# Joining the retention matmul clusters of three more groups, and splitting the last group's stores over two queues, in a retention layer followed by a squared-ReLU MLP

## The chip, the cores and the metric

The kernel runs on one core of one Trainium2 chip. The metric is the device time of one launch in microseconds (us), as the median over runs. A span is the part of one profiled execution between its first and last recorded work.

## What is computed

The first half is retention, that is, attention without a softmax and with a causal decay mask; the second half is an MLP with a squared ReLU. All inputs and the output are float32.

```python
# q, k, v: (8, 8, 576, 64); w_in: (512, 2048); w_out: (2048, 512)
scores = (1/sqrt(64)) * q @ k.T                       # per batch and head
gamma  = 1 - 2.0**(-5 - arange(8))                    # one decay per head
D      = where(rel >= 0, gamma**rel, 0)               # rel = row - column
x      = (scores * D) @ v                             # heads joined: (4608, 512)
h      = x @ w_in
out    = (maximum(h, 0)**2) @ w_out                   # (4608, 512)
```

## The kernel before

**Tiling.** The 4608 rows are cut into 36 units of 128 rows. A "full" unit is one chunk of 128 positions of one batch; a "tail" unit holds the last 64 positions of two batches. Two units make a group, so there are 18 groups, numbered 0 to 17; groups 8 and 17 are tails. Units 0 to 7 (groups 0 to 3, `PAIRED = 8`) take another path, with transposes on TensorE; from group 4 on, the two projections `kq` of a unit (k and q, cast to fp16 on POOL at L371 and L382) are transposed by a DMA into the tile `kqT` (L400, in `fx2`). The values are cast and scaled on POOL into `v16` (L387).

**Retention.** For each group there are four sets of small 64x64 matmuls on TensorE, all issued by the helper `quad` (L357): the scores (tile `psc`), the sum of k times v over the chunk, for the running state (`psS`), the contribution of the earlier state to the output (`psO`, from `kqT` and the states `R` and `Rm`; `emit_out1`), and the contribution of the chunk itself (`psO`, from the masked scores `rT` and `v`; `emit_out2`). VectorE masks the scores into `rT` (L692), updates the state (L711 to L717 and L461), and scales `psO` into `xT`, the input of the MLP (L751).

These sets stand on TensorE in two ways, which `add_ret` chooses by `joined(g)`, that is, `JOIN <= g < last_g` with `JOIN = 7`.

- Not joined: one cluster `fa` (scores and sums of the group), and later one cluster `fb` (`emit_out1`, an explicit `nc.tensor.drain()`, `emit_out2`).
- Joined: one cluster `f1` (`emit_out1` of group g and the scores of group g+1), and later one cluster `f2` (the sums of group g+1 and `emit_out2` of group g). So the scores of group g+1, and with them the transposed tiles `kqT` of its two units, are needed when the output of group g is made.

**MLP.** The first product is 64 matmuls of 128x256 per group (L875, tile `ph`). ScalarE applies the ReLU (L883, `rl`), ScalarE or VectorE squares it (L893, L895, `gT`). The second product is made from seven half-size products instead of eight (L972, tiles `po`; 56 matmuls of 128x256 per group), with sums of `gT` on VectorE (L945, `gS`) and sums of the results on ScalarE and VectorE (L985, L995, L1013, L1024, L1046) into the output tile `o`. The output of a group is stored by `store` on SP's queue (L845, L849); loads of q, k and v are on SP's queue as well (L298, L301, L304). A load needs one of five slots `ld`, which its casts free.

**Order.** The order of all instructions comes from a planner in the kernel (`Schedule`). Each task has an engine, a key (a lower key goes first among ready tasks), an assumed duration, dependencies and buffers. The planner plays through the program with these durations and emits the instructions in the order of its starts; on the chip each engine then works through its own list in that order and waits at semaphores. A changed duration, key or dependency can therefore reorder everything that follows. The key of the casts of a group depends on `JOIN` too: they are due one or two times `L = 32` ahead of the group.

**The last group.** Group 17 stores four halves of 128x256, each as two DMAs of 64 rows (one for each of two batches): the halves that the tasks `d11` and `d22` finish on ACT's queue, those of `c12` and `d21` on SP's. `d21` (L995) is the last to finish.

Of the kernel before, what the change touches and what calls it, by code (L numbers as in the profile page):

```python
# [15 lines left out]
class Schedule:  # L16
# [7 lines left out]
    def add(self, eng, key, dur, fn, deps=(), acq=(), after=None, lag=0.0):  # L24
        t = dict(eng=eng, key=key, dur=dur, fn=fn, acq=acq, n=len(self.tasks), users=[], free=[], lag=lag,
                 left=len(deps), ready=0.0, lat=self.LAT[eng] if after is None else after)
        for d in deps:
            d["users"].append(t)
        self.tasks.append(t)
        return t  # L30
# [73 lines left out]
def kernel(  # L104
# [9 lines left out]
    nc = tc.nc  # L114
    B, H, S, D = q.shape
    DM, DFF = w_in.shape
    assert (B, H, S, D, DM, DFF) == (8, 8, 576, 64, 512, 2048)
    P = 128
# [114 lines left out]
    WT_KEY = 96  # L233
    URGENT = 40
    SQ_LATE = (1, 4, 6)
    JOIN = 7
    LAG = {"k4": 0.7, "q4": 0.5}
    LAG_T, LAG_O = 1.5, 5.0
    PAIRED = 8
# [3 lines left out]
    add = sched.add  # L243
# [105 lines left out]
    T = {}  # L349
# [15 lines left out]
    def add_unit(u, base):  # L365

        kind, b, c = units[u]
        tail = [tail_dec] if kind == "tail" else []

        def sorted_cast(op, out_, in_):  # L370
            op(out=out_.rearrange("p (n b a d) -> p n b a d", n=2, b=2, a=2),  # L371
               in_=in_.rearrange("p (a n b) d -> p n b a d", n=2, a=2))

        def fk():
            t = tile_of["kq", u] = cast.tile([P, 2, H * D], FP16, name="kq16", tag="kq16")
            sorted_cast(nc.gpsimd.tensor_copy, t[:, 0], tile_of["k32", u])

        def fq():
            if kind == "tail":
                sorted_cast(nc.gpsimd.tensor_copy, tile_of["kq", u][:, 1], tile_of["q32", u])  # L380
            else:
                nc.gpsimd.tensor_copy(out=tile_of["kq", u][:, 1].rearrange("p (t a d) -> p a t d", t=4, a=2),  # L382
                                      in_=tile_of["q32", u].rearrange("p (a t) d -> p a t d", a=2))

        def fv():
            t = tile_of["v16", u] = cast.tile([P, H, D], FP16, name="v16", tag="v16")
            nc.gpsimd.tensor_tensor(  # L387
                out=t, in0=tile_of["v32", u],
                in1=vdec[kind].rearrange("p (h o) -> p h o", o=1).to_broadcast([P, H, D]), op=ALU.mult)
        ck = add("POOL", base, 0.65, fk, deps=[loaded["k", u]], acq=("kq",))  # L390
        cq = add("POOL", base + 1, 0.62, fq, deps=[loaded["q", u], ck])
        cv = add("POOL", base + 2, 1.1, fv, deps=[loaded["v", u]] + tail, acq=("v16",))
        for what, t in (("k", ck), ("v", cv)):
            for w in gate.get((what, u), []):
                sched.need(w, t)
        T["casts", u] = [ck, cq, cv]
        sched.free("ld", [ck, cq, cv])
        def fx2():
            t = tile_of["kqT", u] = work.tile([P, 2 * NP, P], FP16, name="kqT", tag="kqT", bufs=6)
            nc.sync.dma_start_transpose(out=t, in_=tile_of["kq", u].rearrange("p x n -> p (x n)"))  # L400
        T["kqT", u] = [add("SP", -1, 2.7, fx2, deps=[ck, cq], acq=("kqT",), after=3.0, lag=LAG_T)]

    def add_unit_pair(u, base):

# [180 lines left out]
    def units_of(g):  # L585
        return sorted(groups[g])
# [4 lines left out]
    def base_of(g):  # L591
        return (units_of(g)[0] - len(groups[g])) * L - EARLY
# [81 lines left out]
    def joined(g):  # L674

        return JOIN <= g < last_g

# [83 lines left out]
    def add_casts(g):  # L761
        for u in units_of(g):
            if u < PAIRED:
                if u % 2 == 0:
                    add_unit_pair(u, base_of(g) - 5)
                continue
            add_unit(u, base_of(g) - L * (2 if g > JOIN else 1) + 4 * (u - units_of(g)[0]))

# [50 lines left out]
    HF, HM = NF // 2, DM // 2  # L819
# [18 lines left out]
                sched.need(w, p)  # L838
    wT_done = {7: t3, 6: t2, 5: t1, 4: t4}

    def store(u, o, lo=0, hi=DM, eng=nc.sync):
        kind, b, c = units[u]
        if kind == "full":
            r0 = b * S + c * P
            eng.dma_start(out=out[r0:r0 + P, lo:hi], in_=o[:, lo:hi])  # L845
        else:
            for i in range(2):
                r0 = (b + i) * S + 512
                eng.dma_start(out=out[r0:r0 + 64, lo:hi], in_=o[i * 64:(i + 1) * 64, lo:hi])  # L849


    T["ff2"] = []
# [4 lines left out]
    def add_ff(g):  # L857
# [45 lines left out]
        if STRASSEN <= g:  # L903
            add_strassen(g, us, base2, sq)
            return
        ends = []
        for s, u in enumerate(us):
            end = base2 + NF * (s + 1)
            f2 = []
            late = g == 0 and s == 1  # L910
            for fi in range(NF):
                def f(fi=fi, s=s, u=u):
                    if fi == 0:
                        tile_of["po", u] = ps_ff.tile([P, DM], FP32, name="po", tag="ff")
                    nc.tensor.matmul(tile_of["po", u], lhsT=tile_of["g", g][:, fi, s * P:(s + 1) * P],  # L915
                                     rhs=w_out16[:, fi, :], start=(fi == 0), stop=(fi == NF - 1))
                f2.append(add("PE", 95.9 + fi / 1000 if late else base2 + NF * s + fi, 0.216, f, deps=[sq[fi // nf]] + wcast[4 + fi // 4] + f2[-1:],
                              acq=("ff",) if fi == 0 else ()))

            def fo(u=u):  # L920
                tile_of["o", u] = o_pool.tile([P, DM], FP32, name="o", tag="o")
                nc.scalar.copy(out=tile_of["o", u], in_=tile_of["po", u])
            oc = add("ACT", end + 1, 0.59, fo, deps=[f2[-1]], acq=("o",))
            sched.free("ff", [oc])
            st = add("SP", -0.5, 0.7, lambda u=u: store(u, tile_of["o", u]), deps=[oc], after=2.5, lag=LAG_O)
            sched.free("o", [st])
            ends.append(f2[-1])
# [3 lines left out]
    def add_strassen(g, us, base, sq):  # L931
# [56 lines left out]
        def o_tile(u):  # L988
            if ("o", u) not in tile_of:
                tile_of["o", u] = o_pool.tile([P, DM], FP32, name="o", tag="o")  # L990
            return tile_of["o", u]

        def on_dve_add(u, half, x, name, key, deps, acq=()):
            def f():
                nc.vector.tensor_tensor(out=o_tile(u)[:, half * HM:(half + 1) * HM], in0=bank(x), in1=tile_of[name, g],  # L995
                                        op=ALU.add)
            return add("DVE", base + key - URGENT, 0.42, f, deps=deps, acq=acq)

        if g == last_g:
# [17 lines left out]
            d11 = on_dve_add(uA, 0, "b", "p1", 17, [p2, c1, c12])  # L1017
# [8 lines left out]
            d22 = on_dve_add(uB, 1, "c", "u4", 21, [p7, c4], ("o",))  # L1026
            d7 = add("DVE", base + 22, 0.42, f7, deps=[d22, c2], acq=("p1",))
            d21 = on_dve_add(uB, 0, "e", "p1", 29, [p4, d7])
        else:
# [6 lines left out]
            d11 = on_dve_add(uA, 0, "b", "p1", 17, [p2, c1], ("o",))  # L1036
# [4 lines left out]
            d22 = on_dve_add(uB, 1, "c", "u4", 22, [p7, c4], ("o",))  # L1041
# [14 lines left out]
        for u, ds in ((uA, [d11, c12]), (uB, [d22, d21])):  # L1056
            if g < last_g:
                st = [add("SP", -0.5, 0.7, lambda u=u: store(u, o_tile(u)), deps=ds, after=2.5, lag=LAG_O if g < last_g - 1 else 0.0)]
            else:
                st = []  # L1060
                for d in ds:
                    lo = 0 if d in (d11, d21) else HM
                    eng = ("ACT", base + 25.1, 0.05) if d is d11 or d is d22 else ("SP", -0.5, 0.05)
                    st.append(add(*eng, lambda u=u, lo=lo, eng=eng: store(u, o_tile(u), lo, lo + HM,
                                                                          nc.scalar if eng[0] == "ACT" else nc.sync),
                                  deps=[d], after=2.5))
            sched.free("o", st)

    for g in range(len(groups)):
# [42 lines left out]
```

## Time and profile before

| | |
|---|---|
| Median of 4 runs | 290.21 us (290.06 to 290.32) |
| The profiled execution: its own time | 290.32 us |
| The profiled execution: span | 288.6 us |
| TensorE (PE) busy | 280.6 us, 97% |
| PE weight load (PEld) busy | 236.1 us, 82% |
| ScalarE (ACT) busy | 187.9 us, 65% |
| VectorE (DVE) busy | 179.0 us, 62% |
| GpSimd (POOL) busy | 89.0 us, 31% |

The profiled execution's own time is 1.7 us above its span: work that lies before and after what is recorded. Busy times of TensorE are modelled at their ends, since matmuls overlap. In a chain or a timeline the first two columns are the start and the length in us; then come the engine, the line and what was written from what; "x8" is the number of instructions.

### The profile page before, as it was taken

How to read it: one execution, taken by the hardware profiler on the slowest of the kernel's cores; microseconds unless marked ns; L12 is line 12 of the kernel's file. 1: busy time of each engine (PE TensorE's matmuls, PEld its weight loads, DVE VectorE, ACT ScalarE, POOL GpSimd, SP SyncE). 2: the span in 40 equal slices, each digit the busy share in tenths (PEclk: the TensorE clock that was granted, in tenths of full speed). 3: DMA queues.
4: the chain of work that ended last, by engine and by line, in shares of the span. 5: the costliest groups of instructions: out<-in, count | busy, mean ns of one | idle time of the engine just before them, and what ended most of it. 6: DMA issues, size and time to landing. Idle time of an engine off the chain costs nothing.

```text
span 288.6 us, 10134 instructions
## 1 busy us (share of the span) xinstructions
PE 280.6 (97%) x4346; PEld 236.1 (82%) x4346; DVE 179.0 (62%) x341; ACT 187.9 (65%) x363; POOL 89.0 (31%) x124
## 2 busy tenths in 40 slices
PE   6999999999999999999999999999999999999994
PEld 2568767888888888888888888888888888888883
DVE  3772389757574848737677676666457656265632
ACT  5559975767575767567676757584867585847830
POOL 5660046433514336252525154262433000000000
PEclk9999999999999999999999999999999999999999
DMA  7999999998989898999989799979989010202004
GB/s 201 275 208 206 249 287 273 196 236 145 237 204 228 179 232 200 210 196 240 155 216 200 169 180 224 214 174 234 174 209 193 2 73 2 75 2 75 0 9 139
DMA packets 122156, 49.94 MB, mean 173 GB/s; under 512 B 94720, under 2 KB 117760, under 8 KB 122112
## 3 DMA queue, kind: packets, MB, share of 16 engines
q1 hardware_dynamic: 117568, 44.84, 70.8%
q0 software_dynamic: 4224, 4.19, 8.8%
q8 instruction: 34, 0.56, 0.8%
q10 hardware_dynamic: 320, 0.26, 0.4%
q14 instruction: 10, 0.08, 0.1%
HBM read 36.70 MB, written 9.44 MB: 160 GB/s over the span
## 4 chain that ended last, share of the span: by engine, by line
PE 91%; DMA 3%; POOL 2%; issue 2%; DVE 0%; POOLq 0%; DVEq 0%
PE ph L875 44%; PE po L972 36%; PE psO L357 4%; DMA w_in<-in_moe_w_in_dram 3%; PE po L915 2%; PE psc L357 2%; PE psS L357 2%; PE psT L439 1%; POOL mask L216 0%; POOL vx L420 0%; POOL w_in L331 0%; DVE o L995 0%; POOL mask_full L208 0%; POOL mask_tail L208 0%; DVE p L1024 0%
## 5 line engine op out<-in xcount | busy, mean ns | idle before, releaser
L875 PE MATMUL ph<-xT,w_in 128*128 128x256 f16 x1152 | 138.4, 273 | 0.1
L875 PEld LDWEIGHTS <-w_in 128*128 128x128 f16 x1152 | 111.3, 98 | 14.5 <-DMA w_in<-in_moe_w_in_dram 0.4
L883 ACT ACTIVATE rl<-ph 128x512 f16<-128x512 f32 x144 | 84.5, 588 | 56.2 <-PE ph L875 53.7
L893 ACT ACTIVATE gT<-rl 128x512 f16<-128x512 f16 x118 | 74.7, 633 | 3.4
L972 PEld LDWEIGHTS <-gS 128*128 128x128 f16 x544 | 51.7, 98 | 6.5
L972 PE MATMUL po<-wT,gS 128*128 128x256 f16 x408 | 55.9, 273 | 0.0
L972 PEld LDWEIGHTS <-gT 128*128 128x128 f16 x408 | 39.7, 98 | 4.7
L945 DVE TENSOR_TENSOR gS<-gT,gS 128x512 f16<-128x512 f16 (+1 forms) x51 | 31.9, 626 | 18.3 <-ACT gT L893 17.7
L972 PE MATMUL po<-w_out,gT 128*128 128x256 f16 x272 | 36.7, 273 | 0.0
L371 POOL CAST kq<-k 128x512 f16<-128x512 f32 x28 | 20.7, 740 | 45.2 <-DMA k<-in_k_dram 41.3
L387 POOL TENSOR_TENSOR v<-v,vdec_full 128x512 f16<-128x512 f32 x24 | 26.7, 1112 | 23.4 <-DMA v<-in_v_dram 18.8
L945 DVE TENSOR_TENSOR gS<-gT 128x1024 f16<-128x1024 f16 x34 | 26.6, 782 | 10.8 <-ACT gT L893 10.7
L382 POOL CAST kq<-q 128x512 f16<-128x512 f32 x24 | 16.1, 672 | 31.2 <-DMA q<-in_q_dram 31.1
L895 DVE TENSOR_TENSOR gT<-rl 128x512 f16<-128x512 f16 x26 | 11.9, 458 | 21.5 <-ACT rl L883 21.5
L995 DVE TENSOR_TENSOR o<-po,u 128x256 f32<-128x256 f32 x33 | 13.9, 422 | 17.1 <-PE po L972 8.4
L985 ACT COPY u<-po 128x256 f32<-128x256 f32 x34 | 12.5, 369 | 13.6 <-PE po L972 13.5
L751 DVE TENSOR_TENSOR xT<-psO,gam_full 128x512 f16<-128x512 f32 x28 | 18.0, 684 | 3.7 <-PE psO L357 3.5
L995 DVE TENSOR_TENSOR o<-po,p 128x256 f32<-128x256 f32 x18 | 7.6, 424 | 19.2 <-ACT u L985 10.0
L972 PE MATMUL po<-w_out,gS 128*128 128x256 f16 x136 | 17.8, 273 | 0.0
L972 PE MATMUL po<-wT,gT 128*128 128x256 f16 x136 | 17.6, 273 | 0.0
L692 DVE TENSOR_TENSOR rT<-psc,mask_full 128x512 f16<-128x512 f32 x24 | 15.7, 683 | 2.1 <-PE psc L357 2.0
L461 DVE TENSOR_TENSOR R<-stmp,dec 128x512 f16<-128x512 f32 (+1 forms) x18 | 12.1, 672 | 0.4
(82 smaller groups left out, 220.4 us busy)
## 6 DMA issues: line engine op xcount, KB each, us to landing
out_dram<-o SPq DMA_DIRECT2D x32, 256.0 KB, 2.6
k<-in_k_dram SPq DMA_DIRECT2D x24, 256.0 KB, 5.2
q<-in_q_dram SPq DMA_DIRECT2D x96, 64.0 KB, 3.3
v<-in_v_dram SPq DMA_DIRECT2D x24, 256.0 KB, 4.2
pair<-in_k_dram SPq DMA_DIRECT2D x4, 512.0 KB, 8.0
pair<-in_q_dram SPq DMA_DIRECT2D x4, 512.0 KB, 5.5
pair<-in_v_dram SPq DMA_DIRECT2D x4, 512.0 KB, 7.3
w_in<-in_moe_w_in_dram POOLq DMA_DIRECT2D x4, 512.0 KB, 8.9
```

What stands on the lines that cost most here:

```text
L357: t = nc.tensor.matmul(out_, lhsT=lhsT, rhs=rhs, start=start, stop=True, skip_group_check=True, tile_position=(64 * row, 64 * col))
L371: op(out=out_.rearrange("p (n b a d) -> p n b a d", n=2, b=2, a=2), in_=in_.rearrange("p (a n b) d -> p n b a d", n=2, a=2))
L382: nc.gpsimd.tensor_copy(out=tile_of["kq", u][:, 1].rearrange("p (t a d) -> p a t d", t=4, a=2), in_=tile_of["q32", u].rearrange("p (a t) d ...
L387: nc.gpsimd.tensor_tensor(out=t, in0=tile_of["v32", u], in1=vdec[kind].rearrange("p (h o) -> p h o", o=1).to_broadcast([P, H, D]), op=ALU. ...
L692: tile_of["masking", g] = nc.vector.tensor_tensor(out=tile_of["rT", g][:, :, a], in0=tile_of["psc", g][a].rearrange("p (s n i) -> p s n i" ...
L751: nc.vector.tensor_tensor(out=tile_of["x", g].rearrange("p n (s e i) -> p e (n s) i", s=n, e=2)[:, c], in0=y.rearrange("p (o t r) -> p o r ...
L875: nc.tensor.matmul(tile_of["ph", g, fb][:, j, :], lhsT=w_in16[:, m, fi * P:(fi + 1) * P], rhs=tile_of["x", g][:, m, :], start=(m == 0), st ...
L883: nc.scalar.activation(out=t, in_=tile_of["ph", g, fb], func=ACTF.Relu)
L893: nc.scalar.activation(out=t, in_=rl, func=ACTF.Square)
L945: nc.vector.tensor_tensor(out=tile_of["S", g][:, k, sl], in0=in0(sl), in1=in1(sl), op=op)
L972: nc.tensor.matmul(tile_of["pb", g, bank], lhsT=left(i), rhs=right[:, i, :], start=(start and i == 0), stop=(i == HF - 1), skip_group_chec ...
L995: nc.vector.tensor_tensor(out=o_tile(u)[:, half * HM:(half + 1) * HM], in0=bank(x), in1=tile_of[name, g], op=ALU.add)
```

## The change

There are three edits.

1. `JOIN` goes from 7 to 4. Groups 4, 5 and 6 are now joined as well. Three clusters `fa` (of groups 5, 6, 7) and three clusters `fb` (of groups 4, 5, 6) become three `f1` and three `f2`. The same small matmuls are issued in them; three explicit drains are gone. The casts of groups 5, 6 and 7 are keyed earlier by 32.
2. The planner counts a DMA transpose as 2.1 us of SP's time instead of 2.7. The transposes themselves are the same.
3. Each of the last group's four half stores has its first DMA on SP's queue and its second on ACT's, instead of both on one of them. There are eight DMAs as before, four on each queue.

```diff
-    JOIN = 7
+    JOIN = 4
...
-        T["kqT", u] = [add("SP", -1, 2.7, fx2, deps=[ck, cq], acq=("kqT",), after=3.0, lag=LAG_T)]
+        T["kqT", u] = [add("SP", -1, 2.1, fx2, deps=[ck, cq], acq=("kqT",), after=3.0, lag=LAG_T)]
...
-    def store(u, o, lo=0, hi=DM, eng=nc.sync):
+    def store(u, o, lo=0, hi=DM, engs=(nc.sync, nc.sync)):
         kind, b, c = units[u]
         if kind == "full":
             r0 = b * S + c * P
-            eng.dma_start(out=out[r0:r0 + P, lo:hi], in_=o[:, lo:hi])
+            engs[0].dma_start(out=out[r0:r0 + P, lo:hi], in_=o[:, lo:hi])
         else:
             for i in range(2):
                 r0 = (b + i) * S + 512
-                eng.dma_start(out=out[r0:r0 + 64, lo:hi], in_=o[i * 64:(i + 1) * 64, lo:hi])
+                if engs[i]:
+                    engs[i].dma_start(out=out[r0:r0 + 64, lo:hi], in_=o[i * 64:(i + 1) * 64, lo:hi])
...
                 for d in ds:
                     lo = 0 if d in (d11, d21) else HM
-                    eng = ("ACT", base + 25.1, 0.05) if d is d11 or d is d22 else ("SP", -0.5, 0.05)
-                    st.append(add(*eng, lambda u=u, lo=lo, eng=eng: store(u, o_tile(u), lo, lo + HM,
-                                                                          nc.scalar if eng[0] == "ACT" else nc.sync),
-                                  deps=[d], after=2.5))
+                    for i, eng in enumerate((("SP", -0.5, 0.05), ("ACT", base + 25.1, 0.05))):
+                        engs = (nc.sync, None) if i == 0 else (None, nc.scalar)
+                        st.append(add(*eng, lambda u=u, lo=lo, engs=engs: store(u, o_tile(u), lo, lo + HM, engs), deps=[d], after=2.5))
```

## The prediction

> **What bounds the kernel now.** I read the page's busy row and its slices first, then TensorE's waits, then the chain of work that ended last, then TensorE's timeline around the clusters that the change touches, and last SP's and ACT's timelines at the end.
>
> ```profile
> PE 280.6 (97%) x4346; PEld 236.1 (82%) x4346; DVE 179.0 (62%) x341; ACT 187.9 (65%) x363; POOL 89.0 (31%) x124
> PE   6999999999999999999999999999999999999994
> ```
>
> TensorE is busy in all slices but the first and the last. Its waits between 20 and 284 us come back as an empty list, and the chain of that stretch stays on it. So a microsecond is gained only by what TensorE itself does, or by what follows its last matmul. The chain prices a cluster. First group 5, not joined, then groups 7 and 8, joined:
>
> ```profile
> 75.01 1.75 PE po L972 x16
> 76.75 0.38 PE psc L357 x32
> 77.42 0.54 PE po L972 x4
> ...
> 80.14 1.75 PE ph L875 x16
> 82.24 0.57 PE psO L357 x48
> 82.81 0.98 PE po L972 x8
> ...
> 126.01 0.87 PE ph L875 x8
> 127.39 1.85 PE po L972 x16
> 129.24 1.75 PE ph L875 x16
> 131.37 0.40 PE psO L357 x48
> 131.76 2.73 PE ph L875 x24
> ```
>
> A wide matmul streams in 0.1092 us (1.75/16). A cluster costs the gap between the wide matmuls on its two sides, plus what the first wide batch after it takes too long. `fa`: 76.76 to 77.42 is 0.66, and four matmuls in 0.54 instead of 0.44 add 0.10: 0.76. `fb`: 81.89 to 82.81 is 0.92, plus 0.11: 1.03. `f1` (126.88 to 127.39, plus 0.10): 0.61. `f2` (130.99 to 131.76, plus 0.11): 0.88. The timeline shows why `fb` is dear:
>
> ```profile
> 81.95 0.19 PE L357 MATMUL psO<-kqT,R 64*64 64x64 f16 x1
> 82.24 0.32 PE L357 MATMUL psO<-rT,v 64*64 64x64 f16 x16
> ...
> 113.49 0.19 PE L357 MATMUL psO<-kqT,R 64*64 64x64 f16 x1
> 113.51 0.43 PE L357 MATMUL psc<-kqT 64*64 64x64 f16 x32
> ```
>
> The first pair is `fb` of group 5: after the last matmul of `emit_out1` the explicit drain holds the next start back by 0.29. The second is `f1` of group 7: the scores follow after 0.02, since they use other banks and need no drain.
>
> The end, SP's timeline and then ACT's, each for its last issues:
>
> ```profile
> 284.91 1.11 SPq L849 DMA_DIRECT2D out_dram<-o  x2
> 283.12 1.20 ACTq L849 DMA_DIRECT2D out_dram<-o  x2
> 284.36 1.25 ACTq L849 DMA_DIRECT2D out_dram<-o  x2
> ```
>
> The last half (`d21`, 284.45 plus 0.42) is ready at 284.87. SP issues its two DMAs one after the other: the first takes 0.47, the second starts near 285.44, and the tile view gives 2.0 to 2.1 us from an issue to its landing.
>
> **What the Trainium skill says.** "TensorEngine Tiling (Array Packing)", Key Properties: changing the tiling mode drains TensorE. The trace agrees: each way back from 64x64 to full matmuls costs the 0.10 to 0.11 above. Joining leaves two clusters for a group, so this part is not saved. "DMA: Bandwidth & Descriptors", Rules for kernel authors: spreading DMAs over queues gives no bandwidth and saves only the sequencer's issue time. The trace has that time: 0.47 to 0.59 on SP, 0.56 to 0.61 on ACT. "Perfetto Trace Analysis", What "DMA-bound" means: one form is an issuing sequencer that is solid with DMA slices. SP is nearly so from 50 to 80 us here; rival C rests on it. The same page, Optimizing Scalar/DVE Operations: GpSimd and VectorE share an SBUF read port. A `gS` of 128x1024 takes 0.69 alone and 1.40 at 66.74, beside a POOL product at 66.55.
>
> **The change, part by part.**
>
> *Clusters.* Removed: three `fa` at 0.76 (2.28) and three `fb`, of groups 4, 5 and 6, which cost 1.00, 1.03 and 1.04 by the same reading (3.07): 5.35 us. Added: three `f1` at 0.61 and three `f2` at 0.88: 4.47. Gain **0.88**, all on the path, as TensorE has no idle time. Bounds: 0.75 (group 4 has no earlier state, so its clusters are shorter in both forms) and 1.0.
>
> *What the new places ask for.* In the changed program's order, `fa` of group 4 stays, and the wide matmuls between the clusters can be counted: 92 up to `f1` of group 4, 30 up to its `f2`, then 54, 32, 68, 32 and 68. With 0.1092 each, the cluster costs above and 62.64 as the start (62.54 plus the 0.10), `f1` of groups 4 to 7 begin at 72.7, 83.3, 95.7 and 108.2. They need the `kqT` of units 11, 13, 15 and 17 (each the later of a pair). In the trace of before these are issued at 66.39, 77.29, 89.73 and 103.23, and a transpose lands 3.4 to 4.0 (median 3.7) later: 70.1, 81.0, 93.4 and 106.9. **They are in time by 2.6, 2.3, 2.3 and 1.3 without being moved at all.** In SP's new order a k load (0.58, for the tail 1.46) stands ahead of the second transpose of three of these pairs, and stores (0.5 each) go behind it, so it comes at most about a microsecond later than before: still in time. POOL's order there is unchanged, and v of units 11, 13 and 15, which `f2` needs, was cast by 67.6, 78.5 and 91.6, against `f2` at 76.6, 87.4 and 99.8. So nothing is charged; if this cover fails, `f1` waits on TensorE with all wide matmuls behind it.
>
> *VectorE's hand-over.* `f2` waits for the masks of the next group: two of 0.64, that is 1.29, with 3.3 us (30 wide matmuls) for them in the tightest place, group 4. After `f2` of group 4, 22 wide matmuls (2.40 us) precede the first `ph` that needs its `xT`; before, that lead was over 9 us. The two `xT` take 1.28 together. With one or two `gS` ahead of them, at 0.69 to 1.40, the wait lies between 0 and about 0.5. I take 0, because the `gS` can run while `f2` does; both ends go into the range. Joined groups 7 to 16 run today with no TensorE wait, with the same banks held.
>
> *Transposes at 2.1.* A planner's number: no instruction changes, and what it moves is counted above. Later `f1` have more lead, as the transposes then run ahead of need.
>
> *Stores.* The four DMAs on ACT and four on SP remain. SP now also waits for `d11` and `d22`, and ACT for `c12` and `d21`; behind these waits stand only further last stores, since ACT's last copy (L1013) is already done. ACT's part of `d22` (ready 284.01) would be issued by 284.65, so it is free at 284.87. Both DMAs of `d21` then start near 284.91 instead of 284.91 and 285.44. Gain **0.5**. Bounds: 0 (they share 16 engines, and the second lands when it did) and 0.6.
>
> *Sum.* 0.88 + 0.5 = 1.38. The profiled execution took 290.32, so 288.94; its time is 0.11 above the median 290.21, against which the sum gives 288.83. I say **288.9**.
>
> **The rivals.**
>
> *A, the forecast (75%): 288.9*, by itself 288.5 to 289.3.
>
> *D (11%): the stores gain nothing*, because the last landing is set by what the engines do with 128 KB at once, not by the second issue. The DMA share is only 0.5 to 0.85 between 285 and 287 us, which speaks against it. 290.21 - 0.88 = 289.3.
>
> *B (7%): small VectorE stalls.* At `f2` of group 4 the plan leaves less than before, and POOL's casts of unit 13 fall in it. Two stalls of 0.4 take 0.8 of 1.38: 289.6, which is about no change. Against it: VectorE is 62% busy.
>
> *C (7%), slower: the transposes become the bound.* From 50 to 80 us SP issues almost without a pause, and the 16 DMA engines' share is 1.0. If the k load ahead of a transpose (256 KB, 1.3 us at the stretch's 207 GB/s) and slow q loads (3.4 instead of 2.1 us of SP, both seen) add up, `f1` stands and TensorE with it. It decides once the transposes come more than 2.3 us later than before; the gain is gone at 3.7, and it is slower by over 0.2% from about 4.3. At 5 us late: 2.7 of waits, 290.21 - 1.38 + 2.7 = 291.5. Against it: SP's list up to unit 13 is almost the same, so only something not seen in the trace makes it so late. That the change doesn't join anything is ruled out by the built order.
>
> **How the numbers follow.** About 0.2% (0.58 us) is what can be told from no change here. Faster by more than that are A and D, 86%; within it B, 7%; slower C, 7%. The range of 288.4 to 289.7 takes A with the bounds of the clusters, the hand-over and the stores, and most of D and B; C stays out.
>
> **What would show it.** Right: in the chain, clusters near 0.61 and 0.88 for groups 4 to 6, no pause of 0.29 after `emit_out1`, TensorE's waits still empty, last issues of SP and ACT both near 0.04 after the last `o`, and the end 0.5 nearer to it. Wrong: a TensorE wait for `kqT` near 73, 83, 96 or 108 us (C), or for `xT` near 80 us (B), or the tail from the last `o` to the end still 3.7 us (D).

## The result and the profile after

| | before | after |
|---|---|---|
| Median, us | 290.30 (52 runs, 289.88 to 291.49) | 291.40 (32 runs, 289.89 to 294.76) |
| The profiled execution: own time | 290.32 | 291.77 |
| The profiled execution: span | 288.6 | 290.1 |
| Last `o` written, from the span's start | 284.87 | 286.44 |

The ratio of after to before is **1.0034**, with an interval of 1.0022 to 1.0046: slower by a third of a per cent, about 1 us. The change was forecast to gain 1.4. (Ratios here leave out disturbed runs, so they aren't the quotients of the medians.) After scatters more than before.

The busy row, TensorE's slices and the chain's shares from the page of after:

```profile
PE 281.4 (97%) x4346; PEld 236.0 (81%) x4346; DVE 178.7 (62%) x341; ACT 188.4 (65%) x363; POOL 89.1 (31%) x124
PE   7999999999999997999999999999999999999994
...
PE 57%; DMA 19%; SPq 13%; DVE 3%; POOL 2%; issue 2%; ACT 1%; POOLq 0%; DVEq 0%
```

The busy row is nearly that of before. The slices show one new 7, the sixteenth, from 108.8 to 116.0 us. The chain has changed most: TensorE held 91% of it before, now 57%, and DMA with SP's issuing hold 32%. TensorE's waits over the whole span (total, times, longest) name what it waits for:

```profile
PE psc L357 <- DMA kqT<-kq: 1.8, 2, 1.6
```

Its timeline shows the two places. They are the scores in `f1` of group 7 and in `f1` of group 8; the bracket gives the idle time and what ended it:

```profile
108.53 0.30 PE L357 MATMUL psc<-kqT 64*64 64x64 f16 x16
110.46 0.32 PE L357 MATMUL psc<-kqT 64*64 64x64 f16 x16 [1.63 <-DMA kqT<-kq]
...
122.93 0.30 PE L357 MATMUL psc<-kqT 64*64 64x64 f16 x16
123.40 0.32 PE L357 MATMUL psc<-kqT 64*64 64x64 f16 x16 [0.17 <-DMA kqT<-kq]
```

The first unit's 16 scores run, the second unit's `kqT` isn't there yet, and all wide matmuls stand behind it. By the prediction's reading (the gap between wide matmuls plus the first batch's excess) these clusters cost 2.42 and 0.97 instead of 0.60. SP's timeline has the transpose that group 7 waits for, of unit 17:

```profile
103.08 1.33 SPq L400 DMA_TRANSPOSE kqT<-kq  x1
104.46 0.58 SPq L301 DMA_DIRECT2D k<-in_k_dram  x1
105.16 1.52 SPq L400 DMA_TRANSPOSE kqT<-kq  x1
```

It is issued at 105.16 (103.23 before), and its scores begin at 110.46: 5.3 us later.

The clusters of the newly joined groups are as forecast. Group 5 in TensorE's timeline, `f1` and then `f2`:

```profile
82.27 1.26 PE L876 MATMUL ph<-xT,w_in 128*128 128x256 f16 x10
83.61 0.43 PE L357 MATMUL psc<-kqT 64*64 64x64 f16 x32
83.97 1.05 PE L973 MATMUL po<-w_out,gS 128*128 128x256 f16 x8
...
85.72 1.91 PE L876 MATMUL ph<-xT,w_in 128*128 128x256 f16 x16
87.56 0.45 PE L357 MATMUL psS<-v,kq 64*64 64x64 f16 x32
...
88.34 0.72 PE L876 MATMUL ph<-xT,w_in 128*128 128x256 f16 x5
```

The ten `ph` end at 82.27 + 10 x 0.1092 = 83.36 and the next wide matmul starts at 83.97: 0.61 from these rounded starts. The 16 `ph` end at 87.47 and the next starts at 88.34: 0.87. There is no pause of 0.29.

**The books of the profiled execution.** The last `o` is 1.57 later. The six clusters of groups 4 to 6 cost 0.59, 0.85, 0.60, 0.87, 0.71 and 0.88, together 4.50, against 5.35 before: -0.85. `f1` of group 7 adds 1.82 and that of group 8 0.37. One hole of 0.19 at 77.9, where TensorE waits for a `gS`, is new. That is +1.53; the rest, 0.04, is scatter of single clusters. The tail after the last `o` is 0.07 shorter, so the span grows by 1.5.

### The profile page after: what moved, and what is told of

The parts are those of the page before. It is cut to its first block, busy times and chain, and to the rows that moved or that the text cites. A ratio compares the mean times of both kernels' runs of the same rounds, so it can differ in the third digit from the quotient of the medians.

```text
span 290.1 us, 10131 instructions
## 1 busy us (share of the span) xinstructions
PE 281.4 (97%) x4346; PEld 236.0 (81%) x4346; DVE 178.7 (62%) x341; ACT 188.4 (65%) x363; POOL 89.1 (31%) x124
## 4 chain that ended last, share of the span: by engine, by line
PE 57%; DMA 19%; SPq 13%; DVE 3%; POOL 2%; issue 2%; ACT 1%; POOLq 0%; DVEq 0%
PE ph L876 27%; PE po L973 25%; DMA pair<-in_v_dram 6%; SPq L298 5%; DMA w_out<-in_moe_w_out_dram 5%; DMA k<-in_k_dram 3%; DMA kqT<-kq 3%; DMA q<-in_q_dram 2%; SPq L316 2%; PE psO L357 2%; SPq L304 2%; SPq L400 2%; SPq L301 1%; PE psS L357 1%; DMA v<-in_v_dram 1%
## 5 line engine op out<-in xcount | busy, mean ns | idle before, releaser
L876 PE MATMUL ph<-xT,w_in 128*128 128x256 f16 x1152 | 136.4, 273 | 0.0
L946 DVE TENSOR_TENSOR gS<-gT,gS 128x512 f16<-128x512 f16 (+1 forms) x51 | 31.0, 607 | 20.3 <-ACT gT L894 19.6
L387 POOL TENSOR_TENSOR v<-v,vdec_full 128x512 f16<-128x512 f32 x24 | 27.6, 1150 | 23.9 <-DMA v<-in_v_dram 19.9
L371 POOL CAST kq<-k 128x512 f16<-128x512 f32 x28 | 19.2, 687 | 29.6 <-DMA k<-in_k_dram 27.6
L986 ACT COPY u<-po 128x256 f32<-128x256 f32 x34 | 12.6, 370 | 20.3 <-PE po L973 20.1
L896 DVE TENSOR_TENSOR gT<-rl 128x512 f16<-128x512 f16 x26 | 12.6, 483 | 19.3 <-ACT rl L884 19.3
```

What stands on the lines that cost most here:

```text
L387: nc.gpsimd.tensor_tensor(out=t, in0=tile_of["v32", u], in1=vdec[kind].rearrange("p (h o) -> p h o", o=1).to_broadcast([P, H, D]), op=ALU. ...
L876: nc.tensor.matmul(tile_of["ph", g, fb][:, j, :], lhsT=w_in16[:, m, fi * P:(fi + 1) * P], rhs=tile_of["x", g][:, m, :], start=(m == 0), st ...
L946: nc.vector.tensor_tensor(out=tile_of["S", g][:, k, sl], in0=in0(sl), in1=in1(sl), op=op)
```

## The experiments

All were timed beside the kernel before. The edits are against before or after, as named.

### Which edit loses: each alone

**Stores alone** (edit 3 on the kernel before; here against after, with edits 1 and 2 taken back):

```diff
-    JOIN = 4
+    JOIN = 7
...
-        T["kqT", u] = [add("SP", -1, 2.1, fx2, ...
+        T["kqT", u] = [add("SP", -1, 2.7, fx2, ...
```

> The kernel before with the third edit alone: the last group's half stores with one DMA on each queue. Theory T (late transposes make the changed kernel slower, the stores are nearly neutral): 290.1 to 290.3, ratio 0.999 to 1.000, and a tail from the last o to the end within 0.1 us of the 3.73 of before, as in the changed kernel's 3.66. Rival S (the forecast's store gain is there and was hidden): 289.8, ratio 0.998, tail about 3.2.

Measured: 0.9992 (0.9983 to 1.0002), about 0.2 us, and not told from nothing. The tail from its last `o` to the end is 3.6. Up to the end this is the program of before, so its profile is a second execution of the same order; it is used below.

**Transposes at 2.1 alone** (edit 2 on the kernel before):

```diff
-        T["kqT", u] = [add("SP", -1, 2.7, fx2, ...
+        T["kqT", u] = [add("SP", -1, 2.1, fx2, ...
```

> The kernel before with the second edit alone: a transpose counted 2.1 instead of 2.7, JOIN stays 7. SP's order becomes nearly that of the changed kernel (a k load ahead of the second transpose of a pair), but f1 and fa stand as late on TensorE as before up to group 7. Theory T (it is the early place of f1 that finds the transposes late): no TensorE wait for kqT up to group 7, at most a small one at group 8, 290.2 to 290.5, ratio 1.000 to 1.001. Rival O (SP's new order itself delays everything): 291 or more, with waits for kqT.

Measured: **1.0031** (1.0017 to 1.0045), the whole loss of the joint change, without a group joined. TensorE's timeline in `f1` of group 8:

```profile
121.77 0.30 PE L357 MATMUL psc<-kqT 64*64 64x64 f16 x16
123.26 0.32 PE L357 MATMUL psc<-kqT 64*64 64x64 f16 x16 [1.19 <-DMA kqT<-kq]
```

That cluster began at 126.72 before and begins at 121.52 now, while the transpose of unit 19 went from 115.2 to 119.6. The planner's number moved need and supply towards each other: from 11.5 us between issue and `f1` to 1.9. The place of the wait is as theory T expected, but its size isn't: the time is that of rival O, by which SP's new order itself costs. The same edit with `f1` held, below, decides between the two.

**Joining alone** (edit 1 on the kernel before, transposes still counted 2.7):

```diff
-    JOIN = 7
+    JOIN = 4
```

> The kernel before with the first edit alone: JOIN 4, a transpose still counted 2.7. The planner then puts f1 of groups 4 to 8 about 1 to 4.4 us of TensorE work later than the changed kernel does (for group 7 by 3.5). Theory T: little or no wait for kqT, and the clusters' 0.9 shows: 289.3 to 289.8, ratio 0.997 to 0.998, runs close together. Rival V (the joined clusters or VectorE's hand-over cost more than read, whatever the transposes do): 291 or more. Rival I (the plan has idle time of TensorE in it, and the chip follows it): 291.0 to 292.

Measured: 1.0006 (0.9995 to 1.0018). No wait for `kqT` at all, and yet no gain. TensorE's timeline shows another hole:

```profile
75.27 1.25 PE L972 MATMUL po<-wT,gS 128*128 128x256 f16 x10
77.72 0.61 PE L972 MATMUL po<-wT,gS 128*128 128x256 f16 x4 [1.20 <-DVE gS L945]
```

This order, against the expectation, asks for a `gS` before VectorE has made it; in its profile the gaps of 1.36 here and 0.40 near 94.6 outweigh 0.88. So edit 1 in this order gains nothing, for a reason of its own: rival B's mechanism, with a larger size. After hasn't this hole (0.19 in its place), so edit 2 took it away and brought the transposes' in.

### What makes the transposes late

**Stores made thin** (after; the stores of units 2 to 9 write 16 of 128 rows):

```diff
+            n = 16 if 2 <= u <= 9 else P
-            engs[0].dma_start(out=out[r0:r0 + P, lo:hi], in_=o[:, lo:hi])
+            engs[0].dma_start(out=out[r0:r0 + n, lo:hi], in_=o[0:n, lo:hi])
```

> The changed kernel, where the stores of units 2 to 9 write 16 of their 128 rows (so the output misses 112 rows of each of these units). SP issues the same DMAs in the same order; 1.8 MB less goes through the 16 DMA engines between about 56 and 111 us. Theory T in the form that the 16 engines are the bound (what stands ahead of a transpose in their rings makes it late): the wait of 1.6 at f1 of group 7 shrinks below 0.5, 289.6 to 290.4, ratio 0.998 to 1.000. Theory T in the form that SP's issuing is the bound: the wait stays, 291 to 292.

Measured: 1.0024 (1.0008 to 1.004), not told from after's 1.0034, and `f1` of group 7 still waits 0.95. So the loss doesn't hang on the stores' bytes alone; the wait is shorter than after's 1.63, and neither of the two expected cases fits well.

**v loads made thin** (after; the loads of v for units 10 to 15, 18 and 19 bring 16 of 128 rows, and their cast reads the tile of k, so that the casts and the number of DMAs stay):

```diff
+                    m = 16 if name == "v" and 10 <= u <= 19 else P
-                    nc.sync.dma_start(out=x, in_=src[b, :, c * P:(c + 1) * P, :].rearrange("h p d -> p h d"))
+                    nc.sync.dma_start(out=x[0:m], in_=src[b, :, c * P:c * P + m, :].rearrange("h p d -> p h d"))
```

> The changed kernel, where the v loads of units 10 to 15, 18 and 19 bring 16 of 128 rows and the cast to v16 reads the k tile in their place (so the output of these units is not retention's). SP issues the same number of DMAs in the same order; 1.8 MB less goes through the 16 DMA engines between 59 and 117 us. If the engines' rings make the transposes late: landing 3.4 to 4.0 again, wait for kqT below 0.4, 289.6 to 290.2, ratio 0.997 to 0.999. If SP's issue time does: the second transpose of group 8 is still issued near 105, the wait stays above 1, 291 or more.

Measured: **0.9972** (0.996 to 0.9984). The loss has become a gain of 0.8 us, with SP's list as long as before and 1.8 MB less to move. But the edit does more than take bytes away: the cast to `v16` no longer waits for its load. POOL's waits for v between 55 and 125 us, for after and then for this kernel:

```profile
POOL v L387 <- DMA v<-in_v_dram: 10.4, 8, 2.9
```

```profile
POOL v L388 <- DMA v<-in_v_dram: 1.7, 3, 0.7
```

POOL also makes the casts that the transposes wait for, so the missing bytes and the freed POOL are not told apart. Nor does the profile show how the gain came. It is of an execution of 290.7, above this kernel's median of 289.9, and `f1` of group 7 still waits 1.00 there. (The tile view's median landing between 50 and 130 us, 3.1 against 4.6 in after, rests on five landings here, all of first transposes of a pair; `f1` waits for the second ones.)

The Trainium skill says in "DMA: Bandwidth & Descriptors", Queues, rings and completion order, that each DMA engine consumes its descriptors in the order of the ring, though a later one may finish its write first. A transpose on SP's queue would then be taken up behind the loads issued ahead of it. The runs agree in part: unit 17 landed 5.3 us after its issue with a k load 0.70 ahead of it (after), and 3.5 with a store of the same size 0.62 ahead (stores alone). But unit 15 of after, with its k load 0.74 ahead, took 3.4. What sets a single landing stays open.

### Is it the lead of `f1`, and can the gain be had?

If the transposes come when they come, `f1` must ask later. `add_ret` can hold it back in the planner by `lag`; TensorE then does wide matmuls first.

**`f1` of groups 7 and 8 held back** (after):

```diff
-                     acq=("prO", "prS", "ff", "ff", "ff", "ff"))
+                     acq=("prO", "prS", "ff", "ff", "ff", "ff"), lag=6.0 if g in (7, 8) else 0.0)
```

> The changed kernel, where the planner holds f1 of groups 7 and 8 back by 6 us (lag=6.0 for these two). SP's order up to the second transpose of group 9 is that of the changed kernel, word for word; on TensorE f1 of group 7 stands 5.5 us and f1 of group 8 4.8 us of wide matmuls later. Theory T (the place of f1 against the transposes decides): no wait for kqT at groups 7 and 8, at most 0.3 in all at groups 4 to 6, and the clusters' 0.9 shows: 289.4 to 289.9, ratio 0.996 to 0.998, runs as close together as those of before. Rival P (SP's new order with the loads behind the transposes is what costs, wherever f1 stands): 290.8 or more.

Measured: 1.0001 (0.9982 to 1.002). The two waits are gone, and the loss with them, but the gain isn't there: the profile has a wait of 0.9 at 96.80, in `f1` of group 6.

**`f1` of groups 5 to 8 held back** (after; `lag={5: 2.0, 6: 2.0, 7: 4.0, 8: 6.0}.get(g, 0.0)` at the same place):

> As the last, but f1 of groups 5, 6, 7 and 8 are held back by 2, 2, 4 and 6 us in the plan: 1.8, 2.2, 4.4 and 5.3 us of TensorE work later than in the changed kernel. Theory T: no wait for kqT anywhere in most runs, 289.3 to 289.7, ratio 0.996 to 0.998, no worse than the last. Rival H (a later f1 leaves VectorE too little time before the next group's first product): a new wait on xT or gS of 0.5 to 1, 290.0 to 290.8.

Measured: 0.9993 (0.9971 to 1.0016). The waits again moved on. The profile is of this kernel's slowest execution, 293.05 with a median of 290.32, so the sizes are not typical. TensorE's list of waits, and the timeline in `f1` of group 9, the first group without a lag (the other wait is at 226.92):

```profile
PE psc L357 <- DMA kqT<-kq: 2.6, 2, 1.4
```

```profile
137.33 0.32 PE L357 MATMUL psc<-kqT 64*64 64x64 f16 x16 [1.25 <-DMA kqT<-kq]
```

**One pair only: joining from group 6** (edit 1 with `JOIN = 6`, transposes at 2.7):

```diff
-    JOIN = 7
+    JOIN = 6
```

> The kernel before with JOIN 6 and a transpose still counted 2.7: one more group joined, not three. SP's order is that of before but for the k load ahead of the second transpose of group 8. Theory T: one pair of clusters is 0.3 shorter and f1 of group 7 stands where it did, so no new wait: 290.0 to 290.4 against 290.4, ratio 0.9985 to 1.0. Rival G (joining earlier groups always makes a hole in TensorE's order, as for JOIN 4): a wait on gS or kqT of over 0.5, 290.6 or more.

Measured: 0.9989 (0.9981 to 0.9997): 0.3 us for one pair joined, a third of 0.88, with no wait for `kqT` in the profile (and one of 0.2 for a `gS`).

**Transposes at 2.1, `f1` held** (edit 2 alone with `lag={7: 3.0, 8: 7.0, 9: 7.0, 10: 5.0}.get(g, 0.0)`):

> The kernel before with a transpose counted 2.1 (the edit that alone cost 0.31%), where the planner holds f1 of groups 7 to 10 back by 3, 7, 7 and 5 us, so that these stand on TensorE where they did before, or up to 1.8 us later. SP's order keeps the k loads ahead of the second transposes. Theory T2 (the transposes come at the pace of the DMA engines, a pair in 12 to 13 us, and what costs is only that f1 asks for them faster): no wait for kqT, ratio 0.999 to 1.001, runs as close together as those of before. Rival P (SP's order of loads and transposes costs by itself): ratio 1.002 or more with waits for kqT.

Measured: 0.9997 (0.9984 to 1.001), no wait for `kqT`. The same edit 2 cost 0.31% with `f1` unheld. So it isn't the transposes' number, nor SP's order that comes with it, that costs by itself, but that it lets `f1` move up.

**After, paced over all groups concerned**:

```diff
-                     acq=("prO", "prS", "ff", "ff", "ff", "ff"))
+                     acq=("prO", "prS", "ff", "ff", "ff", "ff"), lag={5: 2.0, 6: 3.0, 7: 4.5, 8: 6.0, 9: 6.0, 10: 4.0}.get(g, 0.0))
```

> The changed kernel with all its three edits, where the planner holds f1 of groups 5 to 10 back by 2, 3, 4.5, 6, 6 and 4 us: f1 of groups 7 to 10 then stand where they did before (93.4, 106.9, 121.6 and 134.5 us of TensorE work against 94.1, 107.6, 121.9 and 135.2), and those of groups 5 and 6 1.8 and 2.2 us later than in the changed kernel. Theory T2: the clusters' 0.9 shows without waits, ratio 0.9965 to 0.998, 289.4 to 289.9. Rival H (with three more groups joined, a wait turns up somewhere else, as at group 9 when only groups 5 to 8 were held): ratio 0.999 or more.

Measured: **0.9961** (0.9949 to 0.9973), median 289.54 against 290.61: 1.1 us faster than before. This beats both kernels. Its list of TensorE's waits has only the three of the start left, the largest of them there in every kernel:

```profile
PE warm L256 <- DVE wT L163: 1.3, 1, 1.3
PE psT L439 <- DVE kx L424: 0.5, 1, 0.5
PE psS L357 <- POOL vx L420: 0.4, 1, 0.4
```

The chain between 70 and 128 us is back on TensorE alone; shares by line, and `f1` of group 7 in it:

```profile
by line: PE po L973 46.0%; PE ph L876 44.8%; PE psO L357 5.2%; PE psc L357 2.3%; PE psS L357 1.9%
...
111.76 0.88 PE po L973 x8
112.63 0.25 PE psO L357 x16
112.88 0.26 PE psc L357 x32
113.14 0.98 PE ph L876 x8
```

All 32 scores go in one piece. The table sets the issue of the later transpose of each pair against the start of the `f1` that needs it (where the wide matmuls ahead of it end); the difference is its lead, in us:

| lead of the transpose before `f1` of group | 4 | 5 | 6 | 7 | 8 | 9 |
|---|---|---|---|---|---|---|
| before (not joined up to 6) | | | | 10.0 | 11.5 | 13.6 |
| edit 2 alone | | | | 6.2 | **1.9** | 6.6 |
| after | 4.6 | 5.1 | **3.0** | **3.1** | **4.7** | 6.7 |
| paced | 5.8 | 7.4 | 5.3 | 7.3 | 8.6 | 9.9 |

Between 50 and 130 us landings take 3.1 to 6.0 in these kernels. The bold leads are the ones at which `f1` waited (in group 6 of after by 0.1); every lead of paced but two is above 6.0, and none waited.

**Paced, joined from group 5** (the edit of paced with `JOIN = 5`) and **joined from 6, with the stores** (join from 6 as above plus edit 3):

> As paced, with JOIN 5 instead of 4: two pairs of clusters shorter, 0.6, and group 4 keeps the long lead before its first MLP product. Theory T2: ratio 0.9975 to 0.9985; better than paced only if the tight start at groups 4 and 5 (a transpose needed 10.6 us of TensorE work after the one before) still costs something there.

> JOIN 6, a transpose counted 2.7, and the last group's stores on both queues. One pair of clusters is 0.3 (0.1%) and join6 gave 0.9989; the stores alone gave 0.9992. If both add: ratio 0.998, 290.0. If the store edit is nothing: 0.999.

Measured: 0.9972 (0.9963 to 0.998) and 0.9984 (0.9976 to 0.9993). With paced's 0.9961 the gain rises with each pair joined: 0.16, 0.28 and 0.39% for one, two and three, all with edit 3. The intervals of neighbours overlap; those of one and three don't. A pair is worth about 0.11 to 0.12%, 0.33 us, where the prediction's 0.88 for three makes 0.29. One pair with the stores against one pair without (0.9984 against 0.9989) leaves the stores 0.15 us, within both intervals.

## Why the prediction was wrong, point by point

**What bounds the kernel: right.** TensorE sets the time; each wait on it shows in the span.

**Clusters, 0.88: right.** 0.85 in the profile of after, and paced reaches 1.1 us with the stores in it.

**"They are in time by 2.6, 2.3, 2.3 and 1.3 without being moved at all", and in the new order "at most about a microsecond later": this step failed.** The needs were right (`f1` forecast at 72.7, 83.3, 95.7, 108.2; measured 72.5, 83.4, 95.8, 108.3). The arrivals were not. Unit 17 was forecast at 106.9 and came at 110.4, 3.5 later, in two terms:

*The issue, 1.9 of it.* SP issues it at 105.16 in after (its lines are above). Before, and then the second execution of the same order, the kernel with the stores alone:

```profile
102.09 0.58 SPq L845 DMA_DIRECT2D out_dram<-o  x1
103.23 1.27 SPq L400 DMA_TRANSPOSE kqT<-kq  x1
```

```profile
103.70 0.52 SPq L845 DMA_DIRECT2D out_dram<-o  x1
104.32 1.32 SPq L400 DMA_TRANSPOSE kqT<-kq  x1
```

So 1.1 of the 1.9 is within what one execution differs from another, and the other 0.8 is about what the prediction gave the k load ahead. The step read one execution's times as fixed.

*The landing, 1.6 of it.* The prediction used 3.4 to 4.0, median 3.7. That line of the tile view rests on two of before's 28 transposes, at 165 and 178 us; the view gives a landing only where no record of its semaphore is missing. For the old order 3.7 was not too short, which is luck. The trace's own records of this one landing (16 for a DMA) are whole: it came at 106.36 before and at 107.78 in the second execution, 3.1 and 3.5 after the issue, and both times ahead of 108.2. What failed is carrying the landing over to the new order. The tile view of unit 17 alone, for after and then for the kernel joined from group 6:

```profile
DMA to landing us min/median/max: 5.3/5.3/5.3
```

```profile
DMA to landing us min/median/max: 3.2/3.2/3.2
```

Both have the k load ahead, 0.70 and 1.41 us before. Over all fourteen profiles, by the same records, unit 17 took 5.0 to 6.0 in the nine with the k load 0.7 to 0.85 ahead, 3.2, 3.8 and 4.9 in the three with it 1.26 to 1.41 ahead, and 3.1 and 3.5 in the two with a store there instead. The prediction charged that load 0.58 of SP's time and put its effect on the landing at nothing. This is one transpose compared over kernels, and not a rule, as unit 15 shows (above).

**"Later `f1` have more lead": the opposite.** Edit 2 alone shows it: the lead of group 8 fell from 11.5 to 1.9. The prediction listed the needs up to group 7 and argued the rest; group 8, which the joining doesn't touch, stands 4 us earlier in after than before. Over groups 4 to 8 of after, TensorE's work asks for a pair every 10.8 to 12.6 us, and SP issues one every 10.4 to 14.5: 50.1 us for the four steps against 48.3 asked (the wait taken off). So the lead runs down, and waits come where it is used up; this fits that holding `f1` of two or four groups only moved the wait. What sets SP's pace no run isolates.

**Hand-over of VectorE, 0: nearly right.** 0.19 in after, inside its bounds. In the order of edit 1 alone it was 1.4.

**Stores, 0.5: the term was mis-sized.** The mechanism came as described. ACT's and SP's last issues in after (each last of its queue's timeline):

```profile
286.47 0.47 SPq L850 DMA_DIRECT2D out_dram<-o  x1
```

```profile
286.48 0.52 ACTq L850 DMA_DIRECT2D out_dram<-o  x1
```

Both start 0.04 after the last `o`, as forecast. But the end is 3.66 after it, against 3.73. By stretches of half a microsecond (the last two numbers are the DMA share and GB/s), after and then before:

```profile
288.00:288.50 0.50, 0.00 (x0) 0.00 (x0) 0.00 (x0) 0.00 (x0) 0.00 (x0) 1.00 0.35 82
288.50:289.00 0.50, 0.00 (x0) 0.00 (x0) 0.00 (x0) 0.00 (x0) 0.00 (x0) 1.00 0.00 0
```

```profile
286.50:287.00 0.50, 0.00 (x0) 0.00 (x0) 0.00 (x0) 0.00 (x0) 0.00 (x0) 1.00 0.75 178
287.00:287.50 0.50, 0.00 (x0) 0.00 (x0) 0.00 (x0) 0.00 (x0) 0.00 (x0) 0.97 0.04 8
```

Taking each last stretch as busy as the one ahead of it (0.72 for after, 287.5 to 288.0), the bytes stop near 287.0 before and 288.25 after, that is 2.15 and 1.8 us after the last `o`. But then 1.6 us pass to the end of the span before, and 1.85 after, so most of the 0.35 doesn't arrive. What fills that time the trace doesn't name. In paced the end is 3.57 after its last `o` (284.23 to 287.8), and the timed runs with and without the edit put the gain at 0.15 to 0.2 us; the forecast 0.5 lies at the very edge of the interval of the stores alone. Rival D's price for it, nothing, is nearer.

**The rivals.** C names the case that happened, `f1` standing for late transposes: its sign, a wait near 108 us, came, and the k load ahead that it named is the one above. Its figures fit by luck. It put the time at 291.5 for transposes 5 us late; 291.4 came with 3.5. Its break-even, 3.7 us of lateness, counts from leads of 2.3, while the prediction's own smallest lead is 1.3, at unit 17; from there it is 2.7. What spoke against it, that SP's list up to unit 13 hardly changes, was beside the point, since the waits are at units 17 and 19. Given a lead of 1.3 and a landing time seen on two of 28 transposes, it deserved far more than 7%.

## What to carry to other kernels

When a change makes the bounding engine ask earlier for what DMA brings, write down for every later request the lead between issue and need, and set it against the longest landing of that same stretch, from more than one execution; look at how many landings a median rests on and where they lie, and don't carry it over to an order that puts other transfers ahead. If supply and demand have nearly the same period, curing one wait moves it to the next request, so hold back the requests over the whole stretch. A planner's assumed duration is not free to change: it moved the need of group 8 by 5 us with only the order of instructions altered, and alone cost 0.31%.

## What the runs showed of the hardware

- The landing of one kind of DMA transpose spreads from 3.1 to 6.0 us between 50 and 130 us of these kernels, where the DMA engines are nearly full (a share of 0.95 to 0.98 between 60 and 110 us in after); the same list, executed twice, issued one transpose at 103.2 and at 104.3.
- The same transpose landed 5.0 to 6.0 us after its issue in nine profiles with a load of 256 KB issued 0.7 to 0.85 us ahead of it on its queue, and 3.1 and 3.5 in two with a store of 256 KB there; taking 1.8 MB out of earlier stores left a wait of 0.95.
- Some 1.6 to 1.85 us pass at the end of the span after the last DMA activity, and a last byte that came 0.35 earlier shortened the tail by 0.07 only.
